# The chunk that spans two batches on the whole array: one group of wide matmuls and a separate multiply of the upper lanes

## The chip, the core and the metric

The program runs on one core of a Trainium2 chip. Its engines work from queues of their own: TensorE (PE, with its weight loads shown as PEld), VectorE (DVE), ScalarE (ACT), GpSimd (POOL) and SyncE (SP), which issues most of the transfers. The metric is the device time of one execution in microseconds (us), lower is better.

## What is computed

The kernel computes a linear attention with random features, and feeds its output to a mixture of experts in which each token goes to one expert. Cut to what matters here:

```python
# q, k, v: (8 batches, 8 heads, 576 tokens, 64); omega: (128 features, 64)
q_p, k_p = phi(q_s), phi(k_s)                     # exp features, 128 per token
kv  = np.einsum('bhsm,bhsd->bhmd', k_p, v)
z   = np.sum(k_p, axis=2)
num = np.einsum('bhsm,bhmd->bhsd', q_p, kv)
den = np.einsum('bhsm,bhm->bhs', q_p, z)[..., None] + 1e-06
attn = num / den
x = attn.transpose(0, 2, 1, 3).reshape(8 * 576, 512)
# then: e = argmax(x @ w_gate); out = gate * sigmoid(...) * (relu(x @ w1[e]) @ w2[e])
```

## The kernel before

**Units.** The attention is done in 32 units. A unit is one head of two batches: 2 times 576 = 1152 tokens, which are 9 chunks of 128. Chunks 0 to 3 belong to the unit's first batch, chunks 5 to 8 to its second, and chunk 4 has 64 tokens of the first and 64 of the second: it spans two batches. Eight units make one of four groups (`j`); after the last unit of a group its tokens are routed to experts, and the expert work is done in items of 128 tokens of one expert (up to 38 of them), whose matmuls stand between those of later units.

**A unit's steps.** `pp` projects keys and queries on PE (L582, 64 rows by 128 columns of the array, in pairs); VectorE takes minima (L604) and makes biases `nb` (L613, L617); ScalarE makes exponentials `ef` (L623); ScalarE and GpSimd split these into a high and a low half-precision part `es` (L644, L646); `kv` sums keys times values on PE (L719); VectorE splits the result into `kvs` (L739, L741); PE multiplies it with the gates (L758, L763); the query features, turned, are `et`. In `kvs` the two batches stand next to each other in the innermost dimension, so that `w[:, :, b]` picks the 81 values of batch b (1 denominator, 64 numerators, 16 gate sums) with a stride of two.

**Numerators.** `attend` (matmuls at L802) multiplies `et` by `kvs` into a PSUM bank `pn`, three products (high-high, high-low, low-high) for each chunk. It is called as two steps: chunks 0 to 4 and chunks 5 to 8. A chunk of one batch takes three matmuls with all 128 columns of weights (128*128 in the rows) and 81 columns streamed. Chunk 4 takes six: three with the weights of its lower 64 tokens against batch 0, written to PSUM lanes 0 to 63, and three with the upper 64 tokens against batch 1, written to lanes 64 to 127. These have 64 columns of weights (128*64 in the rows).

**Division.** `divide` runs on VectorE for each of the two steps: add and scale the denominators (L811), reciprocal (L813), multiply numerators by it into `xf` (L815, 128x400 for chunks 0 to 4, 128x320 for chunks 5 to 8). GpSimd then splits `xf` into rows (L833, L837) and sums gate values (L855; L857 on VectorE at the end of a group).

**Order.** Every step has a number. A table written into the file (`ORDER`) sets the order in which the steps are emitted, a second (`BANKS`) the PSUM bank of each. Each engine executes its instructions in that order and waits where a semaphore says so. The costs given with each step in the code have no effect on that order.

**Items.** An item's hidden layer is at L1586 (`ph`), its second layer at L1617 (`po`, 512 columns streamed), with VectorE's remainder `hl` at L1597 between them. In the last group there are branches for small items, which use 64 columns of weights (L1609).

Of the kernel before, what the change touches and what calls it, by code (L numbers as in the profile page):

```python
# [10 lines left out]
F32 = mybir.dt.float32  # L11
# [4 lines left out]
ALU = mybir.AluOpType  # L16
# [5 lines left out]
P = 128  # L22
B, H, S, D, M = 8, 8, 576, 64, 128
# [3 lines left out]
NSC = 4  # L27
NC = 9
NCV = 10
NP = H // 2  # L30
ROW = DM + 16
KEY = 64
# [3 lines left out]
GW = 2 * NE  # L36
W = 1 + D + GW
# [287 lines left out]
def attention_moe(ctx: ExitStack, tc: tile.TileContext, kqt, kqn, v, om, wg, w1, w2, cf, cm, ci, out):  # L325
    nc = tc.nc
# [44 lines left out]
    def buf(tag, n, shape, dt):  # L371

        n = NBUF.get(tag, n)
        bufs[tag] = n

        def get(i):
            if (tag, i) not in live:
                live[tag, i] = sb.tile([P, *shape], dt, tag=f"{tag}_{i % n}", name=f"{tag}{i}", bufs=1)
            return live[tag, i]

        makers[tag] = get
        return get
# [96 lines left out]
    xl = buf("xlo", 2, [NC * P], F16)  # L479
    rawv = buf("rawv", 2, [NCV, D + 1], F32)  # L480
    vs = buf("vs", 2, [2, NCV, D + 1], F16)
    sqt = buf("sqt", 1, [NC, 2, D], F32)
# [4 lines left out]
    et = buf("et", 2, [2 * NC, P], F16)  # L487
    kvs = buf("kvs", 2, [2, W, 2], F16)
    kvf = buf("kvf", 2, [2, P], F16)
    xf = buf("xf", 2, [NC, D + GW], F32)  # L490
    den = buf("den", 2, [NC], F32)
    xs = buf("xs", 2, [NC, P], F32)
    lga = buf("lga", 2, [NC, GW], F32)

# [38 lines left out]
    def unit(u):  # L533
# [3 lines left out]
        cls = "e" if u < EARLY else "a"  # L537
# [11 lines left out]
        parts = [(g * (NC // 3) * P, (g + 1) * (NC // 3) * P) for g in range(3)] if u == 0 else [(0, NC * P)]  # L549
# [36 lines left out]
        for g in range(G):  # L586
            x = min(g, len(parts) - 1)
            before_ = [("lo", u, x), ("const", "omh")]
            if g or u:
# [3 lines left out]
                tiles=[("xt32", u), ("xn", u)] if whole else [("xhi", u), ("xlo", u)],  # L593
                bank=[(cls, ("pp", 2 * u + i, g), [4, M]) for i in range(2)], cols=3072.0 if whole else 1152.0,
# [3 lines left out]
        for i, nm in enumerate(("k", "q")):  # L598
            n = 2 * u + i
# [27 lines left out]
            for g in range(G):  # L627
# [9 lines left out]
                    tiles=[("nb", n), ("ef", n)], frees=[("pp", n, g)],  # L637
# [32 lines left out]
        if whole:  # L670
# [11 lines left out]
            for g in range(NC // 3):  # L682
                plan.add(
                    ("tq", u, g), ("PE",), 0.33, lambda g=g: turned(g), after=[("ex", qn, g), ("const", "ci")], rank=R + 3,
                    tiles=[("ef", qn)], bank=(cls, ("tq", u, g), [3, P]),
# [3 lines left out]
                    tiles=[("et", u)],  # L689
# [3 lines left out]
                    tiles=[("et", u)], frees=[("tq", u, g)],  # L693
# [11 lines left out]
        def kv_bank():  # L705
            return banks["kv", u][:, 0 : 2 * WIDE * (D + 1)].rearrange("p (b w d) -> p b w d", b=2, w=WIDE)

        def key_values(b):
            kv = kv_bank()
            half = NCV // 2  # L710
            for i in range(half):
# [12 lines left out]
        for b in range(2):  # L724
# [3 lines left out]
                tiles=[("es", slot_es(kn)), ("vs", u)] if fine else [("ef", kn), ("rawv", u)],  # L728
                bank=None if b else (cls, ("kv", u), [512]), cols=1000.0 if fine else 1300.0 * WIDE,
            )  # L730

        def kv_halves(which):
# [14 lines left out]
            tiles=[("kvs", u)],  # L747
# [17 lines left out]
        def gate_halves(which):  # L765
# [12 lines left out]
            tiles=[("kvf", u)],  # L778
# [6 lines left out]
            tiles=[("kvs", u)],  # L785
# [7 lines left out]
        def attend(c0, c1):  # L793
            pn = banks["pn", u, c0]
            kh, kl = (kvs(u)[:, i] for i in range(2))
            eth, etl = et(u)[:, 0:NC], et(u)[:, NC:]
            ops = [(eth, kh), (eth, kl), (etl, kh)]
            for c in range(c0, c1):
                parts = [(0, P, 0 if c < 4 else 1)] if c != 4 else [(0, P // 2, 0), (P // 2, P, 1)]
                for lo, hi, b in parts:  # L800
                    for i, (a, w) in enumerate(ops):
                        nc.tensor.matmul(  # L802
                            pn[lo:hi, c - c0, :], a[:, c, lo:hi], w[:, :, b], start=(i == 0), stop=(i == len(ops) - 1)
                        )

        pr, o = u // 2, (u % 2) * D

        def divide(c0, c1):
            pn = banks["pn", u, c0]
            dn = den(u)[:, c0:c1]  # L810
            nc.vector.tensor_scalar(dn, pn[:, :, 0], EPS * 2.0**LB, 1.0 / SX, ALU.add, ALU.mult)  # L811
            yield
            nc.vector.reciprocal(dn, dn)  # L813
            yield
            nc.vector.tensor_tensor(  # L815
                out=xf(u)[:, c0:c1, :], in0=pn[:, :, 1:], in1=dn.unsqueeze(2).broadcast_to([P, c1 - c0, D + GW]),
                op=ALU.mult,
            )

        for c0, c1, pe, dve in ((0, 5, 0.6, 0.48), (5, NC, 0.42, 0.4)):  # L820
            plan.add(
                ("pn", u, c0), ("PE",), pe, lambda c0=c0, c1=c1: attend(c0, c1), after=[*turned_all, ("gl", u)], rank=R + 5,
                tiles=[("et", u), ("kvs", u)], bank=(cls, ("pn", u, c0), [c1 - c0, W]),
            )
            plan.chain(
                ("xf", u, c0), ("DVE",), (0.07, 0.1, dve), lambda c0=c0, c1=c1: divide(c0, c1), after=[("pn", u, c0)], rank=R + 5,
                tiles=[("xf", u), ("den", u)], frees=[("pn", u, c0)],
            )
# [6 lines left out]
        def lo_half():  # L835
# [7 lines left out]
            tiles=[("xf", u), ("xs", pr)],  # L843
# [6 lines left out]
        def sum_up():  # L850
# [12 lines left out]
            tiles=[("xf", u), ("lga", j)], bank=("e", ("rt", j), [512]) if end else None,  # L863
        )

    def slot_es(n):

        return n // 2 if n < 2 * SPLIT_FROM else n - SPLIT_FROM

    def pair(pr):  # L870
        j, hp = divmod(pr, NP)
        R = 10.0 * (2 * pr + 1) + 7 + GAP * (2 * pr >= H)
        both = [("xl", 2 * pr), ("xl", 2 * pr + 1)]
        plan.add(
            ("rows", pr), ("SP",), 0.45,
            lambda: nc.sync.dma_start(
                rows[j * NC * P : (j + 1) * NC * P, hp * P : (hp + 1) * P].rearrange("(c p) r -> p c r", p=P), xs(pr)
            ),
            after=both, rank=R + 0.5, tiles=[("xs", pr)], dma=1.64,
        )  # L880
# [566 lines left out]
    def cuts_of(n, w, parts=range(NQ)):  # L1447
# [6 lines left out]
        1: [(("ef", FREE + 1), ef), (("ef", FREE + 2), ef), (("et", NSC * H), et), (("et", NSC * H + 1), et)],  # L1454
        2: [(("es", ES), es), (("es", ES + 1), es), (("xs", NSC * NP), xs), (("xs", NSC * NP + 1), xs)],
    }
# [15 lines left out]
    def item(n):  # L1472
# [75 lines left out]
        def gather():  # L1548
# [8 lines left out]
            ("gx", n), "POOL", 1.04, gather, rank=-800.0 + n, tiles=[("gx", n)], dma=0.75,  # L1557
            after=[("gi", gr)] + [("scales", s) for s in range(j + 1)] + [("rows", p) for p in range(NP * (j + 1))],
        )
# [123 lines left out]
    for u in range(NSC * H):  # L1683
        unit(u)
    for pr in range(NSC * NP):
        pair(pr)
# [87 lines left out]
```

## Time and profile before

| what | value |
|---|---|
| time, median of 3 runs | 628.85 us (627.51 to 632.21) |
| the profiled execution's own time | 623.89 us |
| its span, first to last instruction | 622.0 us |
| PE busy | 593.9 us (95%), 8716 matmuls |
| DVE busy | 387.9 us (62%), 1219 instructions |
| ACT busy | 421.6 us (68%) |
| POOL busy | 374.3 us (60%) |
| mean granted clock of TensorE | 0.986 |

The busy time of an engine is the time in which at least one of its instructions is in flight. A matmul is shown from its start until its last result has left the array, and the next one starts long before that; how densely PE works is therefore read from the distance between two starts, not from the length of one. Idle time of an engine that nothing waits for costs nothing.

### The profile page before, as it was taken

Reading aid. Unit: us, or ns where it says so; the run is one execution under the profiler, and the core shown is the slowest. Engines: PE = TensorE matmul, PEld = TensorE weight load, DVE = VectorE, ACT = ScalarE, POOL = GpSimd, SP = SyncE. Lnnn points to the kernel's source line nnn. Section 1 sums busy time; section 2 is a strip of 40 time slices with the busy share of each in tenths; the row PEclk is TensorE's granted clock in tenths of the full one; section 3 lists DMA queues with packets and bytes.
Section 4 is the critical chain, followed back from the end, with each engine's and each line's share of the span. In section 5 each row is a group of like instructions: output and inputs, shape, how many; then the busy total and the mean of one; then the engine's idle time right before and its main releaser. Section 6 shows DMA issues by size and latency. Waiting matters only on the chain. (4 is left out here: it accounts for less than half of the span.)

```text
span 622.0 us, 22247 instructions
## 1 busy us (share of the span) xinstructions
PE 593.9 (95%) x8716; PEld 471.6 (76%) x8716; DVE 387.9 (62%) x1219; ACT 421.6 (68%) x978; POOL 374.3 (60%) x275
## 2 busy tenths in 40 slices
PE   6999987999999899999999999999999999999995
PEld 6999876867786677778877777778867867677764
DVE  4777699866678987647797865543783530351124
ACT  6999999789889688989868787871522521351143
POOL 2265589789976688999788889985322111211203
PEclk9999997899999999999999999999999999999998
DMA  7655689999999999999989998778676647742671
GB/s 269 201 163 167 201 266 210 222 238 268 290 270 249 225 252 209 289 199 230 298 223 260 231 196 200 175 180 212 203 163 215 205 80 215 203 99 55 132 284 50
DMA packets 145888, 129.00 MB, mean 207 GB/s; under 512 B 104270, under 2 KB 127440, under 8 KB 144464
## 3 DMA queue, kind: packets, MB, share of 16 engines
q1 hardware_dynamic: 139760, 107.45, 69.1%
q0 software_dynamic: 5984, 19.72, 10.3%
q8 instruction: 80, 1.31, 0.9%
q14 instruction: 64, 0.52, 0.3%
HBM read 83.86 MB, written 19.30 MB: 166 GB/s over the span
## 5 line engine op out<-in xcount | busy, mean ns | idle before, releaser
L1586 PE MATMUL ph<-xt,w1h 128*128 128x128 f16 (+1 forms) x2432 | 206.8, 218 | 0.8 <-ACTq L1510 0.4
L1586 PE MATMUL ph<-xt,w1l 128*128 128x128 f16 (+1 forms) x1216 | 203.1, 218 | 0.4 <-DVEq L1515 0.4
L1586 PEld LDWEIGHTS <-w1h 128*128 128x128 f16 x2432 | 184.3, 98 | 9.0 <-issue 1.3
L623 ACT ACTIVATE ef<-pp,nb 128x128 f32<-128x128 f32 x576 | 163.0, 394 | 17.3 <-DVE nb L617 13.1
L604 DVE TENSOR_REDUCE pp<-pp 128x3 f32<-128x384 f32 x192 | 102.8, 557 | 33.2 <-PE pp L582 28.2
L1586 PEld LDWEIGHTS <-w1l 128*128 128x128 f16 x1216 | 118.5, 98 | 0.5 <-DVEq L1515 0.5
L646 POOL TENSOR_TENSOR es<-ef,es 128x1152 f16<-128x1152 f32 x44 | 104.5, 2385 | 20.1 <-ACT es L644 13.4
L1597 DVE SCALAR_TENSOR_TENSOR hl<-ph,hh 128x512 f16<-128x512 f32 (+1 forms) x76 | 50.4, 664 | 97.8 <-ACTq L1515 61.4
L1617 PE MATMUL po<-w2h,hl 128*128 128x512 f16 x280 | 106.1, 379 | 1.8 <-DVE hl L1597 1.8
L1617 PE MATMUL po<-w2h,hh 128*128 128x512 f16 x280 | 106.2, 379 | 0.2 <-PE ph L1586 0.2
L1617 PE MATMUL po<-w2l,hh 128*128 128x512 f16 x280 | 106.1, 379 | 0.0
L1549 POOL DMA_INDIRECT gx<-rows,gi x38 | 38.2, 1005 | 104.4 <-ACT os L1672 46.1
L1593 ACT ACTIVATE hh<-ph 128x512 f16<-128x512 f32 (+1 forms) x76 | 44.6, 590 | 83.0 <-PE ph L1586 69.3
L1617 PEld LDWEIGHTS <-hh 128*128 128x128 f16 x560 | 51.3, 98 | 52.7 <-issue 0.3
L516 POOL TENSOR_TENSOR xlo<-xt,xhi 128x1152 f16<-128x1152 f32 x24 | 57.2, 2383 | 10.8 <-ACT xhi L509 8.6
L1617 PEld LDWEIGHTS <-hl 128*128 128x128 f16 x280 | 27.4, 98 | 35.4 <-DVE hl L1597 2.5
L1672 ACT ACTIVATE os<-po,gx 128x512 f32<-128x512 f32 (+1 forms) x34 | 23.4, 687 | 43.8 <-PE po L1617 37.6
L644 ACT CAST es<-ef 128x1152 f16<-128x1152 f32 x44 | 51.5, 1181 | 0.7 <-ACTq L1510 0.2
L802 PE MATMUL pn<-kvs,et 128*128 128x81 f16 (+1 forms) x960 | 47.5, 204 | 0.9 <-ACT ef L623 0.5
L802 PEld LDWEIGHTS <-et 128*128 128x128 f16 (+1 forms) x960 | 40.5, 101 | 7.6 <-issue 0.5
L582 PE MATMUL pp<-omh,xhi 64*128 64x128 f16 x432 | 42.6, 223 | 2.9 <-ACT ef L623 1.9
L582 PE MATMUL pp<-omh,xlo 64*128 64x128 f16 x432 | 41.1, 222 | 0.7 <-POOL xlo L516 0.7
(193 smaller groups left out, 1059.6 us busy)
## 6 DMA issues: line engine op xcount, KB each, us to landing
r<-w SPq DMA_DIRECT2D x10, 2048.0 KB, 9.0
xt<-kqt SPq DMA_DIRECT2D x32, 576.0 KB, 5.3
xn<-kqn SPq DMA_DIRECT2D x24, 576.0 KB, 5.7
rawv<-v SPq DMA_DIRECT2D x32, 325.0 KB, 5.4
rows<-xs SPq DMA_DIRECT2D x16, 576.0 KB, 6.0
r<-w SPq DMA_DIRECT2D x8, 512.0 KB, 6.3
ef<-w SPq DMA_DIRECT2D x2, 512.0 KB, 3.9
et<-w SPq DMA_DIRECT2D x2, 512.0 KB, 8.0
```

What stands on the lines that cost most here:

```text
L516: lambda t0=t0, t1=t1: nc.gpsimd.tensor_tensor(out=xl(u)[:, t0:t1], in0=xt32(u)[:, t0:t1], in1=xh(u)[:, t0:t1], op=ALU.subtract),
L582: nc.tensor.matmul(banks["pp", 2 * u + i, g][:, c, :], x[r, t], w[r, :], start=(a == 0), stop=(a == len(ops) - 1))
L604: nc.vector.tensor_reduce(out=pp[:, 3, 0:3], in_=pp[:, 0:3, :], op=ALU.min, axis=AX.X)
L623: nc.scalar.activation(ef(n)[:, c, :], banks["pp", n, g][:, c % 3, :], AF.Exp, bias=nb(n)[:, c : c + 1], scale=-SK)
L644: nc.scalar.copy(es(slot_es(n))[:, 0], ef(n))
L646: nc.gpsimd.tensor_tensor(out=es(slot_es(n))[:, 1], in0=ef(n), in1=es(slot_es(n))[:, 0], op=ALU.subtract)
L802: nc.tensor.matmul(pn[lo:hi, c - c0, :], a[:, c, lo:hi], w[:, :, b], start=(i == 0), stop=(i == len(ops) - 1))
L1549: nc.gpsimd.indirect_dma_start(out=gx(n), out_offset=None, in_=rows[0 : (j + 1) * NC * P], in_offset=bass.IndirectOffsetOnAxis(ap=tabs[gr] ...
L1586: nc.tensor.matmul(ph[:, f4, 0:w_], w[qd][:, kk, fo : fo + P], xt(n)[:, x, 0:w_], start=(a == 0), stop=(a == 3 * KC - 1))
L1593: nc.scalar.activation(hh(n)[:, sl, 0:w_], banks["ph", n, g][:, :, 0:w_], AF.Relu)
L1597: nc.vector.scalar_tensor_tensor(out=hl(n)[:, sl, 0:w_], in0=banks["ph", n, g][:, :, 0:w_], scalar=0.0, in1=hh(n)[:, sl, 0:w_], op0=ALU.ma ...
L1617: nc.tensor.matmul(po, x(n)[:, f, :], w[f // 2][:, f % 2, :], start=(f == 0 and a == 0), stop=(f == FC - 1 and a == 2))
```

## The change

From unit 10 on, chunk 4 is no longer cut at lane 64. Its three products use all 128 columns of weights and stream 162 columns, the 81 of both batches, into two neighbouring blocks of the bank: block 4 holds batch 0's result for all 128 lanes, block 5 batch 1's. Half of each block isn't used. The bank grows from 5 blocks to 6, the denominators of the step from 5 to 6, and `den` from 9 to 10. The multiply of chunks 0 to 4 stays as it is and now writes wrong values to lanes 64 to 127 of chunk 4; a second VectorE multiply of 64 lanes by 80 values, from block 5, writes these lanes again. In units 0 to 9 nothing changes. The tables of the order and of the banks are the same.

```diff
+MID = NC // 2
+ABREAST = 10
...
-    den = buf("den", 2, [NC], F32)
+    den = buf("den", 2, [NC + 1], F32)
...
             for c in range(c0, c1):
-                parts = [(0, P, 0 if c < 4 else 1)] if c != 4 else [(0, P // 2, 0), (P // 2, P, 1)]
+                if c == MID and abreast:
+                    for i, (a, w) in enumerate(ops):
+                        nc.tensor.matmul(
+                            pn[:, c - c0 : c - c0 + 2, :], a[:, c], w.rearrange("p w b -> p b w"), start=(i == 0), stop=(i == len(ops) - 1)
+                        )
+                    continue
+                parts = [(0, P, 0 if c < MID else 1)] if c != MID else [(0, P // 2, 0), (P // 2, P, 1)]
...
         pr, o = u // 2, (u % 2) * D
+        abreast = u >= ABREAST
+
+        def blocks(c0, c1):
+            return c1 - c0 + (abreast and c0 <= MID < c1)
 
         def divide(c0, c1):
             pn = banks["pn", u, c0]
-            dn = den(u)[:, c0:c1]
+            n = blocks(c0, c1)
+            dn = den(u)[:, c0 + (c0 > MID) :][:, 0:n]
             nc.vector.tensor_scalar(dn, pn[:, :, 0], EPS * 2.0**LB, 1.0 / SX, ALU.add, ALU.mult)
             yield
             nc.vector.reciprocal(dn, dn)
             yield
             nc.vector.tensor_tensor(
-                out=xf(u)[:, c0:c1, :], in0=pn[:, :, 1:], in1=dn.unsqueeze(2).broadcast_to([P, c1 - c0, D + GW]),
+                out=xf(u)[:, c0:c1, :], in0=pn[:, 0 : c1 - c0, 1:], in1=dn[:, 0 : c1 - c0].unsqueeze(2).broadcast_to([P, c1 - c0, D + GW]),
                 op=ALU.mult,
             )
+            if n > c1 - c0:
+                nc.vector.tensor_tensor(
+                    out=xf(u)[P // 2 :, MID, :], in0=pn[P // 2 :, n - 1, 1:], in1=dn[P // 2 :, n - 1 : n].broadcast_to([P // 2, D + GW]), op=ALU.mult
+                )
...
-                tiles=[("et", u), ("kvs", u)], bank=(cls, ("pn", u, c0), [c1 - c0, W]),
+                tiles=[("et", u), ("kvs", u)], bank=(cls, ("pn", u, c0), [blocks(c0, c1), W]),
```

On PE, the end of unit 10's step for chunks 0 to 4 stands like this before, from the last full chunk to the next step (the first number of a MATMUL row's shape is the lanes that it writes, the second the columns streamed):

```order
L802 LDWEIGHTS et_2328
L802 MATMUL pn_0_2590<-kvs_2212,et_2328 128x81
L802 LDWEIGHTS et_2328
L802 MATMUL pn_0_2590<-kvs_2212,et_2328 64x81
L802 LDWEIGHTS et_2328
L802 MATMUL pn_0_2590<-kvs_2212,et_2328 64x81
...
L802 LDWEIGHTS et_2328
L802 MATMUL pn_0_2590<-kvs_2212,et_2328 64x81
L763 LDWEIGHTS kvf_2555
L763 MATMUL kv_2386<-wgs,kvf_2555 128x32
```

The same place on PE in the changed kernel:

```order
L810 LDWEIGHTS et_2328
L810 MATMUL pn_0_2590<-kvs_2212,et_2328 128x81
L803 LDWEIGHTS et_2328
L803 MATMUL pn_0_2590<-kvs_2212,et_2328 128x162
L803 LDWEIGHTS et_2328
L803 MATMUL pn_0_2590<-kvs_2212,et_2328 128x162
L803 LDWEIGHTS et_2328
L803 MATMUL pn_0_2590<-kvs_2212,et_2328 128x162
L765 LDWEIGHTS kvf_2555
L765 MATMUL kv_2386<-wgs,kvf_2555 128x32
```

Six narrow matmuls with their weight loads have become three wide ones; what stands ahead and behind is the same. Of the 22 changed units, 9 have a projection (L584 of the changed kernel, L582 before, 64 rows of the array) right behind the three, the other 13 an instruction that uses the whole array. On VectorE, the division of the same unit stands like this before (what is in brackets is the engine whose semaphore the instruction waits for):

```order
L811 TENSOR_SCALAR den_2628<-pn_0_2590 128x5 [waits PE_49]
L813 RECIPROCAL den_2628<-den_2628 128x5 [waits DVE_49]
L815 TENSOR_TENSOR xf_2629<-pn_5_2577,den_2628 128x320 [waits Pool_49]
L1597 SCALAR_TENSOR_TENSOR hl_2490<-ph_1_2494,hh_2464 128x512 [waits Activation_49]
L815 TENSOR_TENSOR xf_2629<-pn_0_2590,den_2628 128x400 [waits DVE_49]
L617 SCALAR_TENSOR_TENSOR nb_2479<-pp_2_2558,sqs_2279 128x3
```

And so in the changed kernel:

```order
L824 TENSOR_SCALAR den_2625<-pn_0_2590 128x6 [waits PE_49]
L826 RECIPROCAL den_2625<-den_2625 128x6 [waits DVE_49]
L828 TENSOR_TENSOR xf_2626<-pn_5_2577,den_2625 128x320 [waits Pool_49]
L1614 SCALAR_TENSOR_TENSOR hl_2490<-ph_1_2494,hh_2464 128x512 [waits Activation_49]
L828 TENSOR_TENSOR xf_2626<-pn_0_2590,den_2625 128x400 [waits DVE_49]
L833 TENSOR_TENSOR xf_2626<-pn_0_2590,den_2625 64x80 [waits DVE_49]
L619 SCALAR_TENSOR_TENSOR nb_2479<-pp_2_2558,sqs_2279 128x3
```

One instruction has been put behind the multiply of chunks 0 to 4, and it waits for that multiply to be finished. The order of all else on VectorE is the same, and GpSimd, ScalarE and SyncE have the same instructions in the same order.

## Rows read from the trace of the kernel before

**Rows 1.** The page: busy us, share of the span, instructions.

```profile
PE 593.9 (95%) x8716; PEld 471.6 (76%) x8716; DVE 387.9 (62%) x1219; ACT 421.6 (68%) x978; POOL 374.3 (60%) x275
```

**Rows 2.** Windows: busy us (count) of each engine, PEclk the granted clock.

```profile
100.00:107.00 7.00, 5.11 (x46) 5.01 (x46) 6.86 (x37) 5.78 (x16) 7.00 (x4) 0.74 0.71 193
107.00:113.90 6.90, 6.69 (x73) 5.75 (x71) 5.33 (x23) 5.21 (x15) 3.36 (x3) 0.51 1.01 218
...
120.00:445.00 325.00, 318.99 (x5123) 249.30 (x5122) 228.48 (x760) 258.23 (x591) 266.02 (x189) 1.00 0.97 235
```

**Rows 3.** Waits of PE from 120 to 445 us: total, times, longest.

```profile
PE po L1617 <- DVE hl L1597: 1.8, 1, 1.8
...
PE kv L758 <- DVE nb L617: 1.1, 1, 1.1
PE kv L719 <- POOL es L646: 0.9, 2, 0.6
```

**Rows 4.** Timeline of PE at units 19 and 21: start, us, instructions merged.

```profile
268.03 0.88 PE L802 MATMUL pn<-kvs,et 128*128 128x81 f16 x18
268.84 0.28 PE L1586 MATMUL ph<-xt,w1h 128*128 128x128 f16 x2
...
282.19 0.28 PE L1586 MATMUL ph<-xt,w1h 128*128 128x128 f16 x2
282.30 0.22 PE L1586 MATMUL ph<-xt,w1l 128*128 128x128 f16 x1
282.35 0.28 PE L758 MATMUL kv<-cmt,kvs 128*128 128x128 f16 x2
282.56 0.23 PE L582 MATMUL pp<-omh,xhi 64*128 64x128 f16 x2
...
283.67 0.64 PE L802 MATMUL pn<-kvs,et 128*128 128x81 f16 x12
284.15 0.23 PE L763 MATMUL kv<-wgs,kvf 128*128 128x32 f16 x3
...
286.91 0.87 PE L802 MATMUL pn<-kvs,et 128*128 128x81 f16 x18
287.71 0.23 PE L582 MATMUL pp<-omh,xhi 64*128 64x128 f16 x2
```

**Rows 5.** Groups of VectorE's instructions, 127 to 445 us: busy, mean ns.

```profile
L815 DVE TENSOR_TENSOR xf<-pn,den 128x400 f32<-128x400 f32 x22 | 12.4, 567 | 0.4
L815 DVE TENSOR_TENSOR xf<-pn,den 128x320 f32<-128x320 f32 x22 | 10.6, 484 | 0.4
```

**Rows 6.** The same view, 470 to 475 us: the multiply-like row on 64 lanes.

```profile
L1261 DVE TENSOR_TENSOR r_gid<-r_gid,a_g_a_i_n 64x24 f32<-64x24 f32 x1 | 0.2, 183 | 1.9 <-PE a_g_a_i_n L1257 1.9
```

**Rows 7.** Timeline of VectorE, then of PE, around 202 to 209 us.

```profile
202.22 0.57 DVE L815 TENSOR_TENSOR xf<-pn,den 128x400 f32<-128x400 f32 x1
202.71 0.30 DVE L741 SCALAR_TENSOR_TENSOR kvs<-kv,kvs 128x130 f16<-128x130 f32 x1
202.91 4.12 DVE L857 TENSOR_TENSOR rt<-lga,xf 128x144 f32<-128x144 f32 x1
206.94 0.55 DVE L604 TENSOR_REDUCE pp<-pp 128x3 f32<-128x384 f32 x1
...
206.13 0.38 PE L1617 MATMUL po<-w2l,hh 128*128 128x512 f16 x1
208.35 0.39 PE L1617 MATMUL po<-w2h,hl 128*128 128x512 f16 x1 [1.83 <-DVE hl L1597]
```

**Rows 8.** Timeline of VectorE at the routing after unit 31.

```profile
444.35 0.23 DVE L929 TENSOR_REDUCE r_top<-rt 128x9 f32<-128x72 f32 x1
444.62 0.24 DVE L933 TENSOR_TENSOR rt<-rt,r_top 128x72 f32<-128x72 f32 x1
```

**Rows 9.** Timeline of GpSimd, 204 to 207 and 365 to 371 us.

```profile
204.46 2.38 POOL L516 TENSOR_TENSOR xlo<-xt,xhi 128x1152 f16<-128x1152 f32 x1
...
367.65 2.39 POOL L646 TENSOR_TENSOR es<-ef,es 128x1152 f16<-128x1152 f32 x1
```

## The prediction

> **What bounds the kernel now.** I read the busy shares first, then who waits for whom on PE, then PE's timeline around a changed step. The shares say that PE works 95% of the span and VectorE 62% [rows 1]; in the stretch that holds all changed steps, 120 to 445 us, PE has an instruction in flight for 318.99 of 325 us at full clock, VectorE for 228.48 and GpSimd for 266.02 [rows 2]. So PE is the bound and its order is fixed: an instruction that PE doesn't execute is time won, unless PE then comes early to a wait that another engine ends. The few such waits in this stretch are the second view: 1.8 us on VectorE's `hl`, 1.1 us on VectorE's biases, 0.9 us on GpSimd's `es` in two waits [rows 3]. They are short, but so is all that this change can give; the forecast hangs on them.
>
> **What the six narrow matmuls cost.** A step of one-batch chunks only is 12 matmuls, and PE starts the next step 0.48 us after its first (283.67 to 284.15), so 0.040 us for one of 81 columns. A step with chunk 4 is 18, and lasts 0.81 us before a full-array successor (268.03 to 268.84) and 0.80 before a projection (286.91 to 287.71) [rows 4]. Less the 12 full ones (0.48), the six narrow ones take 0.33 us, far more than six such streams side by side need. Part of it is the change of the array's shape: two matmuls of 128 columns take 0.21 us until a projection on 64 rows starts (282.35 to 282.56), where three among their like take 0.16 (282.19 to 282.35), 0.055 each; so going over to another shape costs 0.21 - 0.11 = 0.10 us [rows 4]. Chunk 4 pays this on the way in and on the way out: 0.20, and 0.13 us of streaming.
>
> [...]
>
> **What the three wide ones cost.** No row has 162 columns. Taken from 81 and 128 columns (0.040 and 0.055 us) the line goes to 0.066; two of 81 one after the other would be 0.080 [rows 4]. I take 0.07, so 0.21 us for three (0.20 to 0.24), the ends being these two. The stride of two in the streamed operand is there before too. Weights are loaded as for a full chunk.
>
> **PE's sum.** In 13 of the 22 changed units the successor uses the whole array: both shape changes go, 0.33 - 0.21 = 0.12 us each, 1.56 us. In 9 a projection follows, and going over to its 64 rows still costs the 0.10: 0.33 - 0.21 - 0.10 = 0.02 us, 0.2 us together. That is 1.8 us off PE's queue. With 0.24 for the three it is 13 x 0.09 - 9 x 0.01 = 1.1 us; if the last shape change hid behind the wide streams and three took 0.20, 22 x 0.13 = 2.9 us.
>
> **VectorE's sum.** One multiply of 64 lanes by 80 values is added in each of 22 units. Multiplies of 400 and 320 values take 567 and 484 ns, 1.04 ns for each further value [rows 5]; a row on 64 lanes with 24 values takes 183 ns [rows 6], so 80 values come to 183 + 56 x 1.04 = 241 ns. The sixth block adds one value each to two small instructions, a few ns. The multiply waits for the one ahead of it: a row that follows unhindered starts some 0.08 us before the end of the one ahead (202.71 against 202.22 + 0.57) [rows 7], one that waits for its predecessor some 0.04 after it (444.62 against 444.35 + 0.23) [rows 8]. So the queue behind gets later by 0.24 + 0.04 = 0.28 us, by 0.36 if the row behind starts without overlap as well; 22 of them are 6.2 to 7.9 us of VectorE's time. Queued behind are minima, biases, `hl` and the splits of weights; for the multiply itself GpSimd's row split waits. No transfer is moved.
>
> [...]
>
> **What of it reaches the end.** VectorE's 6.2 us are spread over 325 us of which it is idle for 96 [rows 2]. PE waits for it at two places only. The longer is at 208.35, where PE waits 1.83 us for `hl`. VectorE sits there 4.12 us in one small addition (L857, from 202.91) and goes on at 206.94, just when GpSimd's `es` and `xlo` have ended (204.46 + 2.38 = 206.84) [rows 7, 9]. That release is GpSimd's: VectorE arriving 0.3 or 0.6 us later in front of it changes nothing, and PE arriving earlier wins nothing. So the savings of units 10 to 15, 4 x 0.12 + 2 x 0.02 = 0.5 us, are gone there. The 1.1 us wait for the biases [rows 3], which comes after unit 17, takes those of units 16 and 17 (0.14) in the same way, if the biases stay where they are. GpSimd, at 82% in this stretch, ends two more waits (0.9 us, the later one on the `es` from 367.65) [rows 2, 3, 9]; between the wait for the biases and that last one units 18 to 26 save 4 x 0.12 + 5 x 0.02 = 0.58 us, of which I count half. Units 27 to 31 save 4 x 0.12 + 0.02 = 0.5 us with nothing behind them but items, and that PE keeps. Together 0.5 + 0.3 = **0.8 us**. The routing after unit 31 gets its input 0.3 us later on VectorE, but items lie in PE's queue meanwhile, and this costs nothing; were that cover gone, it would be 0.3 us.
>
> The sum is against the profiled execution: 623.89 - 0.8 = 623.1 us. The median of the runs is 5.0 us above that execution with the same instructions; I put the same difference on it: 628.85 - 0.8 = **628.0 us**.
>
> **Rivals.**
> - All of PE's saving arrives. Then the waits on VectorE and GpSimd move forward along with PE, since their inputs come from PE's projections. For it: VectorE itself waits for PE at many places. Against: the release at 206.94 is GpSimd's. 628.85 - 1.8 = 627.0 us, at the bound 626.0.
> - VectorE's multiply gets on the path: slower. The place is the stretch between a unit's projection and its exponentials, where `nb` stands behind the added row and ScalarE, then GpSimd, then PE wait in turn. It decides as soon as more than 0.08 us (1.8 / 22) of the 0.28 per unit reaches PE. If half does, 22 x 0.14 - 1.8 = +1.3 us, 630.2; if all does, 6.2 - 1.8 = +4.4 us, 633.3, or 6.1 more with 0.36 (634.9). Against: PE waits for VectorE for 2.9 us in two waits only [rows 3].
> - Narrow was the better shape. In pairs of column tiles the six would stream in 3 x 0.040 = 0.12 us, and three wide ones in 0.21: +0.09 us each, 22 x 0.09 = +2.0 us, 630.9. This holds if the shape changes are hidden behind something; the 0.33 us for six [rows 4] speak against it. [...]
> - The clock. From 107 us the granted clock stands at 0.51 for 6.9 us, after a stretch in which PE was busy 5.11 of 7 us and at 0.74 [rows 2]. Work at half clock for 6.9 us costs 3.4 us. One such stretch more or fewer gives 631.4 or 624.6. It lies ahead of unit 10, in code that isn't changed, and PE isn't as idle again before 445 us.
> - The change does not do what it says if the wide form were to run at less than one column a step; with twice the 0.07, 0.42 us, it would lose 13 x 0.09 + 9 x 0.19 = 2.9 us, 631.7.
>
> **Chances and range.** The forecast 0.52; all arrives 0.18; VectorE on the path 0.18; narrow better or wide slow 0.05; the clock 0.07, half each way. Runs of the same kernel lie 4.7 us apart, and 1% (6.3 us) is about what a measurement of this kernel can tell from no change. No case but the far end of VectorE's comes near it on the slow side, and none on the fast side without help of the clock: faster by over 1% 0.02, within 0.95, slower 0.03. The range goes from 624.8 (one stretch of low clock fewer, or all arriving plus the spread of the runs) to 632.0 (half to two thirds of VectorE's cost arriving).
>
> **What the profile will show.** PE at L803: three wide matmuls some 0.07 us apart, and steps of 0.69 us where 0.81 stood, 0.79 ahead of a projection. PE has 66 matmuls fewer, VectorE 22 instructions more at 0.24 us, 5.3 us of busy time. The wait at 208 us gets longer by about 0.5 us and ends at the same time; from unit 27 on PE is ahead by up to 0.8 us. I am wrong if PE's waits for VectorE's biases or `hl` grow by more than 2 us in total, if the wide matmuls start more than 0.09 us apart, or if the clock falls at another place.

## The result

The changed kernel takes 634.99 us (median of 20 runs, 631.26 to 640.76), the kernel before 627.88 (20 runs). The ratio is 1.0095, 95% interval 1.0076 to 1.0114: about 6 us slower, where 0.8 us faster was forecast. Some executions fall into a slower state whatever the kernel, and every ratio here is estimated without them, so it is not the quotient of the medians.

The profiled execution took 636.24 us (span 634.5). The profile of before that was shown is of an execution 4 us below its median, so the spans of the two profiles lie 12.5 us apart where the medians lie 7.1 apart. A second profile of before (below) shows which of the differences are chance.

First the parts that came out as forecast. Busy shares of the changed kernel (the page's first part; instructions are behind the x):

```profile
PE 596.6 (94%) x8650; PEld 472.6 (74%) x8650; DVE 394.0 (62%) x1241; ACT 422.4 (67%) x978; POOL 373.9 (59%) x275
```

PE has 66 matmuls fewer than in [rows 1], VectorE 22 instructions more. The groups of the added multiply (L833 in the changed kernel) and of the wide matmuls (L803), with the least, median and longest duration in ns:

```profile
L833 DVE TENSOR_TENSOR xf<-pn,den x22: 244/244/245, 131.7 to 448.7; 64x80 f32<-64x80 f32 x22
```
```profile
L803 PE MATMUL pn<-kvs,et x66: 234/237/242, 129.3 to 443.9; 128*128 128x162 f16 x66
```

The multiply takes 244 ns (forecast 241). PE's timeline around a step with chunk 4, which answers to [rows 4]:

```profile
281.96 0.63 PE L810 MATMUL pn<-kvs,et 128*128 128x81 f16 x12
282.43 0.39 PE L803 MATMUL pn<-kvs,et 128*128 128x162 f16 x3
282.65 0.28 PE L1603 MATMUL ph<-xt,w1h 128*128 128x128 f16 x2
```

Twelve full matmuls, three wide ones 0.07 to 0.08 us apart, and the next step 0.69 us after the first (0.69 to 0.74 before the other full-array successors); ahead of a projection, which follows nine times as forecast, it is 0.79 where nothing waits. The prices of PE's instructions were right. The granted clock is at half speed (0.50) for 6.8 us from 108.0 us on, about as in [rows 2], and in this profile once more, for 3.4 us from 261.6 us on (the stretch, its length, busy time and count of each engine, then the clock):

```profile
260.00:270.00 10.00, 9.30 (x131) 7.39 (x132) 6.74 (x23) 6.58 (x17) 7.52 (x5) 0.83 0.92 223
```

The prediction had named a clock that falls at another place as a sign of being wrong, and here is one. In those 3.4 us matmuls of 81 columns start 0.068 us apart and those of 65 columns 0.055, where the medians from 120 to 261 us are 0.040 and 0.029; that is not quite twice, so the stretch can account for 1.7 us of this profile at most; what PE did ahead of it is told in the last section. The rest of the loss is elsewhere. PE's waits from 120 to 445 us (engine, line, waited for: total, times, longest), which answer to [rows 3], and then those of the items' stretch behind:

```profile
PE kv L760 <- DVE nb L619: 1.4, 1, 1.4
PE ph L1603 <- ACT os L1689: 1.0, 1, 1.0
PE pp L584 <- DVE hl L1614: 1.0, 1, 1.0
PE pn L810 <- DVE nb L619: 0.9, 1, 0.9
PE pp L584 <- DVEq L1527: 0.8, 2, 0.5
```
```profile
PE ph L1603 <- issue: 3.8, 4, 1.4
PE ph L1603 <- DMA xt<-gx: 2.0, 2, 1.1
PE ph L1603 <- ACTq L1532: 1.3, 1, 1.3
```

Two things are new. Up to 445 us VectorE (DVE, and DVEq for its queue) now ends seven groups of waits, 5.1 us in all (the four of them shown here are 4.1), where it ended two with 2.9 us; the longest of before, 1.8 us for `hl`, is gone. Behind that, where nothing of the change executes, PE stands for 3.8 us in "issue", which no semaphore explains. I compare two stretches by the start of the same matmul in each timeline: the **units' stretch**, from the projection at 117.0 us to the second-layer product at 444.2 (times of before), and the **items' stretch**, from there to the end of the span. In the shown profile of before they take 327.2 and 177.8 us, in the changed kernel 331.7 and 185.2. Each is one execution, and other profiles of kernels without the change will show how far chance moves these numbers.

### The profile page after: what moved, and what is told of

It is laid out like the page before. It is cut to its first block, busy times and chain, and to the rows that moved or that the text cites. A ratio compares the mean times of both kernels' runs of the same rounds, so it can differ in the third digit from the quotient of the medians.

```text
span 634.5 us, 22136 instructions
## 1 busy us (share of the span) xinstructions
PE 596.6 (94%) x8650; PEld 472.6 (74%) x8650; DVE 394.0 (62%) x1241; ACT 422.4 (67%) x978; POOL 373.9 (59%) x275
## 5 line engine op out<-in xcount | busy, mean ns | idle before, releaser
L584 PE MATMUL pp<-omh,xhi 64*128 64x128 f16 x432 | 43.8, 224 | 4.6 <-DVE hl L1614 1.0
L810 PE MATMUL pn<-kvs,et 128*128 128x81 f16 (+1 forms) x828 | 42.5, 203 | 2.6 <-DVE nb L619 0.9
L584 PEld LDWEIGHTS <-xhi 64*128 64x128 f16 x864 | 33.9, 97 | 12.8 <-issue 4.7
L810 PEld LDWEIGHTS <-et 128*128 128x128 f16 (+1 forms) x828 | 36.6, 99 | 8.1 <-issue 2.6
```

What stands on the lines that cost most here:

```text
L584: nc.tensor.matmul(banks["pp", 2 * u + i, g][:, c, :], x[r, t], w[r, :], start=(a == 0), stop=(a == len(ops) - 1))
L810: nc.tensor.matmul(pn[lo:hi, c - c0, :], a[:, c, lo:hi], w[:, :, b], start=(i == 0), stop=(i == len(ops) - 1))
```

## The experiments

Two theories. A: the 22 multiplies are on the path, in the units. B: the 132 instructions that PE no longer has (66 matmuls, 66 weight loads) move all its later code, and the fetching of instructions then stalls PE at other places. C, chance, is the rival to both.

### The multiplies alone, PE's saving alone

`dve_only` is the kernel before with, behind L815,

```diff
+            if u >= 10 and c0 == 0:
+                nc.vector.tensor_tensor(
+                    out=xf(u)[P // 2 :, 4, :], in0=pn[P // 2 :, 4, 1:], in1=dn[P // 2 :, 4:5].broadcast_to([P // 2, D + GW]), op=ALU.mult
+                )
```

> The kernel before, PE untouched, with only the second multiply of the upper 64 lanes of the middle chunk added in units 10 to 31 (it writes the values that are there already). Theory A, that VectorE's 22 extra instructions are on the path of the units: PE reaches the end of the units (444 us in the trace before) 5 to 7 us later, and the whole is 1.008 to 1.011 of the kernel before. Theory B, that the loss is one of where PE's code lies and not of VectorE: PE's code is the same as before, so the end of the units moves by under 1 us and the whole stays within 0.3%. Theory C, that the two profiles differ by chance: within 0.3% too.

Measured: 1.0081 (1.0049 to 1.0113). The units' stretch takes 333.2 us, the items' 181.3. The interval and the units' stretch are what theory A expects. PE's longest waits for VectorE from 120 to 445 us:

```profile
PE kv L758 <- DVE nb L617: 1.8, 1, 1.8
PE pn L802 <- DVE nb L617: 1.1, 1, 1.1
PE pp L582 <- DVE hl L1601: 1.0, 1, 1.0
```

`pe_only` is the changed kernel without the `if n > c1 - c0:` block (the second multiply).

> The changed kernel without the second multiply: the upper 64 lanes of the middle chunk keep the first batch's quotient in units 10 to 31, so those tokens get wrong values and may be routed to other experts; only the time up to the end of the units is comparable. Theory A: what is left is the saving on PE, so the end of the units comes 0 to 1.8 us earlier than 444 us. Theory B: PE's code is that of the changed kernel, so the end of the units comes as late as there, about 449 us.

Measured, one profile: PE reaches the last step comparable (404.9 us in before) 289.4 us behind the mark at 117; in six profiles of kernels without the change it is 285.1 to 289.0. The forecast saving on PE is not to be seen; neither is the loss of 4 us that the changed kernel has by then (292.1). Behind 405 us it executes other items, so its 655.8 us mean nothing.

### Shifting code

PE's and VectorE's queues begin with a wait of 3.6 and 3.4 us. Drains placed there move the code behind them, and as long as they fit, they hardly delay the first step: with 48 the first matmul starts at 4.98 us (`after_pad48`), without any at 4.89 (the changed kernel). At 0.07 us each, the price that the two kernels below give, 52 of PE's fit. The edit, ahead of the first step:

```diff
+        for _ in range(48):
+            nc.tensor.drain()
         emit(0)
```

`before_pad124` and `after_pad132` have 124 and 132 of them. These don't fit: the first matmul comes 4.8 and 5.3 us later, (3.6 + 4.8) / 124 = 0.07 us for each drain and as much with 132.

The count of 256 in the two expectations below can be read from the traces: from the packet of 16,384 bytes on the instruction queue that starts at 120.70 us in the profile of before to the one at 444.92 there are 40 such packets, and PE executes 10,249 instructions, 256 for each; in the changed kernel (119.61 to 442.05 us) 39 packets and 9905 instructions, 254. From one packet to the next it is 140 to 421 in before, so 256 is a mean.

> The kernel before with 124 drains of PE at the program's start, while PE has nothing to do: its later code lies, in blocks of 256 instructions, where the changed kernel's lies behind unit 31 (132 instructions fewer there). Theory A: no effect, within 0.3% of the kernel before, or up to 0.4 us more for the drains themselves. Theory B: the items' stretch (444 us to the end) gets the stalls of the changed kernel, 1.0 to 1.5 us each with no semaphore behind them, 5 to 9 us in the sum, and the whole is 1.006 to 1.014. Theory C: within 0.3%, with stalls of that kind at places of their own.

> The changed kernel with 132 drains of PE at the start: its later code lies, in blocks of 256 instructions, where that of the kernel before lies behind unit 31. Theory A: no effect, 1.0076 to 1.0114 as the changed kernel. Theory B: the items' stretch loses the stalls without a semaphore, 5 to 8 us, and the whole falls to 0.997 to 1.003 of the kernel before if the units cost nothing, or to about 1.004 if half of the loss lies there. Theory C: as the changed kernel, with stalls at other places.

Measured: 1.0122 (1.0085 to 1.0160) and 1.0104 (1.0071 to 1.0137). I had put the drains' own cost at 0.4 us, which was wrong, so the totals say little; the items' stretch does: 184.0 and 180.8 us, where the unpadded kernels took 177.8 and 185.2. In these two it goes with the code's place and not with the change.

`before_again` is the kernel before, unchanged.

> The kernel before once more, unchanged, for a second profile. If the stalls in the items' stretch (444 us to the end, 177.8 us in the first profile) belong to PE's code position, this profile shows those of the kernels with the same position (0.37, 0.65, 0.36 and 0.67 us at the same matmuls) and the stretch takes 180 to 181.5 us; if they are chance, 177 to 184 us with stalls at other matmuls. Between 117 and 444 us it takes 325 to 328 us and VectorE does not stand for 1.7 us in front of the denominators at 256 us, under either.

Measured: 627.76 us; 328.6 and 179.6 us. Stalls of 0.34, 0.66, 0.35 and 0.52 us stand at the expected matmuls, the last one three further. The first profile of the same kernel has none of the four, so the place of the code alone doesn't fix these short ones. The expectation on VectorE missed: it stood in front of the denominators for 1.9 us here too, and the wait for `hl` at 208 us on which a term of the forecast rested is absent:

```profile
PE ph L1586 <- DVE sqs L527: 1.7, 1, 1.7
PE pn L802 <- DVE nb L617: 1.2, 1, 1.2
PE pp L582 <- DVE hl L1597: 1.0, 1, 1.0
PE kv L758 <- DVE nb L617: 0.8, 1, 0.8
```

`after_pad48`, `after_pad24` and the control `before_pad48` have drains that fit; `before_vpad11` and `before_vpad22` have 11 and 22 of VectorE's.

> The changed kernel with 48 drains of PE at the start, which fit into the 3.6 us in which PE waits there: PE's later code lies 48 instructions on. If PE's code position makes the stalls without a semaphore in the items' stretch, they stand at other matmuls or are of other sizes than 1.2, 1.6, 1.1, 0.5 and 1.5 us, and the stretch differs from 185.2 us by more than 2 us; the stretch from 117 to 444 us stays at 329 to 333 us. If position does nothing, the stalls are as in the changed kernel, and the whole within 0.3% of it.

> The changed kernel with 24 drains of PE at the start in place of 48. If PE's code position sets the stalls in the items' stretch, these stand elsewhere or have other sizes than with 0 and with 48 drains, and the time lies anywhere from 1.002 to 1.011, most likely between those two kernels; with the drains as such as the cause it is half way, 1.006.

> The kernel before with 48 drains of PE at the start, in time that PE waits there anyway. Control for the changed kernel with the same drains, which came out 5 us faster than without them. If the drains help by themselves (a later start, the clock, the transfers), this kernel gains about as much: 0.991 to 0.995. If they work only through the place of PE's code, this kernel has no bad place to leave: 0.997 to 1.004, with the items' stretch at 177 to 184 us.

> The kernel before with 11 drains of VectorE at the program's start, where it waits for 3.4 us anyway: its code lies 11 instructions later, as it does in the changed kernel around unit 20, and it does no more work. Theory A (the extra multiplies are on the path): no effect, within 0.3%. Theory B' (VectorE's code position makes its 1.7 us stall in front of the denominators at 259 us): the stall is here too, the stretch from 210 to 260 us takes 51 to 52 us in place of 48.5 to 49.1, and the whole is 1.003 to 1.006.

> The kernel before with 22 drains of VectorE at the start, where it waits for 3.4 us: its code lies where that of the changed kernel lies behind unit 31, and it does no more work. If VectorE's code position makes the 0.8% that the added multiplies alone cost, this kernel is 1.005 to 1.010; if it is their work in the units, 0.996 to 1.002.

| kernel | ratio to before | units' stretch | items' stretch | lost inside hidden layers |
|---|---|---|---|---|
| changed kernel | 1.0095 (1.0076 to 1.0114) | 331.7 | 185.2 | 6.5 |
| after_pad24 | 1.0089 (1.0057 to 1.0121) | 330.7 | 186.7 | 6.3 |
| after_pad48 | 1.0033 (1.0002 to 1.0064) | 328.6 | 180.2 | 2.4 |
| before_pad48 | 1.0038 (1.0006 to 1.0069) | 327.2 | 186.3 | 3.8 |
| before_vpad11 | 0.9971 (0.9948 to 0.9993) | 327.7 | 186.4 | 3.3 |
| before_vpad22 | 1.0013 (0.9978 to 1.0047) | 324.6 | 181.3 | 2.3 |

48 drains that do nothing take back two thirds of the loss, and before gains nothing from the same 48 (1.0038, the upper half of what was expected; with 48 drains in both, the kernel with the change and the one without it come out alike). `after_pad48`'s units' stretch lies 0.4 us under the expectation. No cost of VectorE's code place is seen, in the units as little as behind. (Both 186.3 and 186.4 hold a late transfer near 593 us, PE waiting 2.5 and 2.8 us for an item's rows `xt`. That wait comes and goes among the profiles, so a single items' stretch is read with care.)

The table's last column leaves such waits out. It adds up, in us, what PE loses between two neighbouring matmuls of one hidden-layer step in the items' stretch, wherever their starts lie over 0.3 us apart, where 0.056 us is regular (0.5 us of it is one wait for VectorE's queue that all of them have). It is 6.5 in the changed kernel, 6.3 with 24 drains and 5.8 in `before_pad124`. In ten profiles whose PE code lies there as before's does, with the change or without it (`after_pad132` 2.8, `wide_split` below 3.0), it is 2.2 to 3.3, and in the first profile of before 0.5. The changed kernel thus loses 3.2 to 4.3 us more than those ten in a stretch where it executes the same work. PE's waits in that stretch that no semaphore explains, 3.8 us above, are 1.0 us in `before_again` and in `after_pad48` these:

```profile
PE ph L1603 <- issue: 1.2, 4, 0.4
```

What the drains move is seen in one step, the same hidden layer of one item, in the changed kernel and with 24 and 48 drains (timelines of PE; first the step's first row, then the row behind the stall):

```profile
498.77 0.28 PE L1603 MATMUL ph<-xt,w1h 128*128 128x128 f16 x2
...
502.33 0.23 PE L1603 MATMUL ph<-xt,w1l 128*128 128x128 f16 x1 [1.40 <-issue]
```
```profile
497.16 0.28 PE L1603 MATMUL ph<-xt,w1h 128*128 128x128 f16 x2
...
500.15 0.23 PE L1603 MATMUL ph<-xt,w1l 128*128 128x128 f16 x1 [1.44 <-issue]
```
```profile
493.96 0.28 PE L1603 MATMUL ph<-xt,w1h 128*128 128x128 f16 x2
...
494.88 0.23 PE L1603 MATMUL ph<-xt,w1l 128*128 128x128 f16 x1 [0.29 <-issue]
```

Counted in the full timelines, the stall stands behind 32, 20 and 8 matmuls of the step: each 24 drains move it 12 matmuls forward, which with their weight loads are 24 instructions. It is tied to a place in PE's code. Each trace also holds a packet of 16,384 bytes on the instruction queue ahead of the stall's end: these land at 500.95, 498.78 and 493.50 us, and PE goes on 1.38, 1.37 and 1.38 us later. PE's last branch instruction stands 1.3 us ahead of the step in all three (497.49, 495.88, 492.69). In these three, how long PE runs dry goes with where the place lies behind the branch: 32 and 20 matmuls in, the packet starts only within the step (500.01, 497.82) and PE loses 1.6 us; 8 in, it starts ahead of it (492.56), and PE loses 0.5. A later step has the same: a stall behind 24 matmuls without drains (551.54 us; it is the row of 1.3 us above, which the profile puts down to ScalarE's queue), behind 12 with 24.

`before_pad124` bears the 256 out in part: its 124 drains and the 132 instructions that the change takes away make 256 together, a packet's mean count, and it has stalls of 1.6 and 1.6 us behind the same matmuls of two steps as the changed kernel (1.1 and 1.5 there), though not the one shown above. That it is the branch which makes a packet late is argued from the three steps; no run tests it by itself.

### The change with the code in its old place

`wide_split` keeps the wide shape and the multiply, but not the fewer instructions:

```diff
-                    for i, (a, w) in enumerate(ops):
-                        nc.tensor.matmul(
-                            pn[:, c - c0 : c - c0 + 2, :], a[:, c], w.rearrange("p w b -> p b w"), start=(i == 0), stop=(i == len(ops) - 1)
-                        )
+                    for b in range(2):
+                        for i, (a, w) in enumerate(ops):
+                            nc.tensor.matmul(pn[:, c - c0 + b, :], a[:, c], w[:, :, b], start=(i == 0), stop=(i == len(ops) - 1))
```

`abreast24_pad48` is the changed kernel with `ABREAST = 24` and 48 drains: 8 units changed, code in place.

> The changed kernel with each whole-array matmul of 162 columns split into two of 81, one for each batch: six matmuls and six weight loads as before, so PE's code lies exactly where that of the kernel before does, while the wide shape and VectorE's second multiply stay. Position theory: the items' stretch is 178 to 181.5 us in place of 185, and the whole 1.002 to 1.008, the cost of the multiplies alone. If the place of the code does nothing and the loss is the multiplies' and the wide shape's: 1.009 and more, with the stretch at 184 to 187 us.

> The change in units 24 to 31 alone, 48 PE instructions fewer, made good by 48 drains in PE's idle start: behind unit 31 its code lies exactly where that of the kernel before does. If the change as such is nearly neutral there, 0.997 to 1.003; if the multiplies cost on every unit what 22 of them cost alone, 8 of them are 1.003, less up to 0.001 for PE's saving.

Measured: 1.0032 (0.9996 to 1.0068) and 0.9985 (0.9950 to 1.0020). `wide_split`'s units' stretch is 329.8 us, its items' stretch 182.9 (1.4 over the expectation; it holds one wait of 1.5 for `xt`). For `abreast24_pad48` they are 328.5 and 184.7, the latter with 2.5 for `xt`. In `wide_split` a step with chunk 4 takes 0.70 to 0.75 us before a full-array successor, as in the changed kernel (0.69 to 0.74), so both have the same saving on PE, and they differ in the place of the code. Six instructions more on PE in each unit, no work less, and 0.63% of the 0.95% are gone (interval about 0.2 to 1.0%, from the intervals of the two): 3.9 us.

### How many multiplies cost how much

`dve_twice` issues the added multiply twice, `dve_early` only in units 10 to 19, `dve_late` only in 20 to 31.

```diff
-            if u >= 10 and c0 == 0:
+            for _ in range(2 if u >= 10 and c0 == 0 else 0):
```

> The kernel before with the second multiply added twice over in units 10 to 31: 44 instructions more on VectorE, 10.6 us of its time, PE untouched. If their work is on the path as the single one's 0.8% says, twice as much is 1.013 to 1.020, and the stretch from 117 to 444 us takes 336 to 340 us in place of 326 to 329. If the single one's cost was position or chance, 1.000 to 1.009.

> The kernel before with the second multiply added in units 10 to 19 alone (10 of the 22). If the cost lies where VectorE is full of the routings' steps (210 to 260 us), 1.005 to 1.008, nearly all of the 1.0081; if every multiply costs the same, 1.0037.

> The kernel before with the second multiply added in units 20 to 31 alone (12 of the 22). If the cost lies in units 10 to 19, 0.999 to 1.002; if every multiply costs the same, 1.0044.

Measured: 1.0087 (1.0056 to 1.0119), 1.0038 (1.0002 to 1.0073), 1.0020 (0.9988 to 1.0052). Double is less than twice single. Early and late don't decide: early is what an even share predicts, but its interval takes in the 1.005 to 1.007 of a cost in units 10 to 19 too, and late stands at the end of the one expectation and holds the other in its interval. A straight line through zero over the five kernels that have 10, 12, 22, 22 and 44 multiplies with PE's code in place (`wide_split` among them, which has PE's saving as well) gives 0.48% for 22, 3.0 us; each fits it within its interval, `dve_only` by a hair not.

The line is a price, not a mechanism, and the profiles don't show an even share. The units' stretch is 335.7 us in `dve_twice`, just under the expected 336 to 340, 331.5 and 330.7 in the other two, and 324.6 to 328.6 in the six profiles without any of the change. One part of it, between two projections that start at 211.5 and 259.5 us in the first profile of before, comes in two lengths (`act_mul` aside): 47.4 to 50.0 us in seven profiles, 50.8 to 52.4 in ten. Two of the ten, `before_again` and `dve_late`, have executed no added multiply by then; the last section tells what happens there. The rest of the units' stretch is 277.2 to 279.8 us in the six without the change and 277.7 to 279.3 in the five that have all of it in all 22 units (the changed kernel, its three with drains, `wide_split`). So with the whole change, the loss up to 444 us is seen at this one place only. The rest is 282.1 in `dve_only` and 284.4 in `dve_twice`, which have the multiplies and not PE's saving (280.5, 279.9 and 280.9 in `dve_early`, `dve_late` and `abreast24_pad48`). That is a hint that the multiplies cost a little everywhere and PE's saving pays for it, but these are single profiles, and no run tests it.

### The multiply on ScalarE

```diff
-                nc.vector.tensor_tensor(
-                    out=xf(u)[P // 2 :, MID, :], in0=pn[P // 2 :, n - 1, 1:], in1=dn[P // 2 :, n - 1 : n].broadcast_to([P // 2, D + GW]), op=ALU.mult
-                )
+                nc.scalar.activation(xf(u)[P // 2 :, MID, :], pn[P // 2 :, n - 1, 1:], AF.Copy, scale=dn[P // 2 :, n - 1 : n])
```

> The changed kernel with the second multiply of the upper 64 lanes done by ScalarE, as a copy with a scale, in place of VectorE. Theory A: VectorE's part of the loss, 3 to 5 us between 117 and 444 us, goes, and ScalarE's 22 copies of 0.25 us cost 0 to 2 us; 1.001 to 1.006 of the kernel before. Theory B: PE's position is that of the changed kernel, so its 3.5 us in the items' stretch stay. Rival: ScalarE then waits for the reciprocal in the middle of its queue and holds up the exponentials behind it; 1.010 and more.

Measured: 1.0442 (1.0391 to 1.0494). The rival, far beyond its price. The stalls in the items' stretch stand behind the same matmuls as in the changed kernel, as theory B says. The copy takes 0.32 us, but ScalarE stands in front of it (waits of ScalarE, 120 to 445 us):

```profile
ACT xf L833 <- DVE xf L828: 16.5, 8, 3.9
ACT xf L833 <- DVE nb L619: 10.7, 4, 4.1
```

No version beats both kernels: only `before_vpad11`, which changes nothing but a start, has its interval below 1, and its sister with 22 drains doesn't.

## Why the prediction was wrong

- **The sum on PE** held in its prices: 0.69 to 0.74 and 0.79 us steps, 0.07 us wide matmuls, nine successors that are projections. That 1.8 us of PE's queue become time was not shown by any run: `pe_only` has no lead, and 3.9 us for the code and 3.0 for the multiplies leave 0.9 of the 6.0 us, well inside the intervals. It stays open.
- **The code behind the change** is the step that failed most. The prediction let units 27 to 31 save 0.5 us "with nothing behind them but items, and that PE keeps", and put the items themselves at nothing; of transfers it said that none is moved. The packets with PE's own code are transfers too, one for some 256 of its instructions, and 132 instructions fewer move all its later code; with 48 drains to move it again the stalls among the items stood elsewhere and were shorter (2.4 us lost in place of 6.5). That the branches there make the difference is an inference. Price 3.9 us (1.4 to 6.5) by the totals, of which the kept profiles show 3.2 to 4.3 in the items' stretch, where the change executes nothing. This was in no rival.
- **"PE waits for it at two places only"** was the step that hid VectorE's 6.2 us. It read a list of PE's waits as the room that VectorE has; a wait that is absent because VectorE is just in time doesn't stand in it. Measured 3.0 us for 22 multiplies. The rival's "if half does" had +3.1 on VectorE's side and a chance of 0.18, but the agreement is luck: it meant half of 0.28 us in each unit, and with the whole change the profiles show the loss at one place, near 256 us. The rival's far end, 634.9 us, meets the measured 635.0 by luck too, since more than half of the loss is the code's. The sign given for VectorE didn't show: PE's waits for the biases and `hl` came to 3.3 us after 2.9, not to 2 more. The list of waits was also short of its second longest, on exponentials that VectorE's biases release:

```profile
PE pp L582 <- ACT ef L623: 1.2, 1, 1.2
```

- **The 0.28 us of one multiply** were too few. The prediction left open whether the row behind it would start without the overlap of 0.08 us (0.36). It does, and starts later still: in the changed kernel the row behind begins 0.01 to 0.03 us after the multiply's end in 20 of 22 units (after a wait in the other two), as in the rows below. That makes up to 0.03 + 0.24 + 0.03 + 0.08 = 0.38 us for each, 8.4 us for 22 in place of 6.2.

```profile
131.10 0.56 DVE L828 TENSOR_TENSOR xf<-pn,den 128x400 f32<-128x400 f32 x1
131.70 0.24 DVE L833 TENSOR_TENSOR xf<-pn,den 64x80 f32<-64x80 f32 x1
131.98 0.17 DVE L619 SCALAR_TENSOR_TENSOR nb<-pp,sqs 128x3 f32<-128x3 f32 x1
```

- **The wait at 208 us.** 0.5 us of PE's saving were given away to a release by GpSimd [rows 7]. Of the profiles without the change only the first shows that wait; the stretch from 166 to 210 us, 44.5 us there, is 42.4 to 43.6 in the five others. A chance event was taken for a fixture.
- **The clock** and **the narrow shape** as rivals: the mark behind the half-speed stretch at 107 us comes at 117.7 us in the changed kernel, 117.0 to 118.2 in the five kernels without the change whose first matmul isn't delayed, so nothing of the loss lies there; the second stretch at half speed, at 261 us, is in the shown profile and, at 265, in `after_pad132`, but `after_pad24`, `after_pad48` and `wide_split` have none between 115 and 445 us. The narrow shape wasn't better: its steps take 0.80 to 0.83 us before a full-array successor where the whole-array steps take 0.69 to 0.75. In the step of before that starts at 268.03 us its matmuls do start in pairs, 0.010 us apart, but 0.13 us lie between the last full one and the first of them, and 0.13 from the last to the successor, where 0.040 is regular: the shape changes are not hidden.

In sum: +3.9 us code, +3.0 us VectorE, PE's saving unresolved, against +6.0 measured. The first two are estimates from different runs, and their sum is no more exact than their intervals.

## What to carry over

Taking 132 instructions out of PE, the bound of this program, moved its later code, and that alone was worth about 0.6% (0.2 to 1.0%): before a change under 1% is judged, shift the code by some drains in an idle start (24 and 48 gave 1.0089 and 1.0033) and compare at an equal place. VectorE's 30% of idle time was no cover by itself (22 multiplies cost 3.0 us); ask at which instruction such an engine is just in time. And a wait that a term rests on should be seen in two profiles.

## What was unexpected of the hardware

**VectorE late beside a gather and a scatter of GpSimd.** At 256 us VectorE's denominators wait for PE's `pn`. In the first profile of before, then in `dve_only` (timeline; POOL's DMA_INDIRECT rows are the gather and the scatter):

```profile
255.03 0.64 PE L802 MATMUL pn<-kvs,et 128*128 128x81 f16 x12
255.71 0.16 DVE L811 TENSOR_SCALAR den<-pn 128x4 f32<-128x4 f32 x1 [2.75 <-issue]
255.71 0.99 POOL L1549 DMA_INDIRECT gx<-rows,gi  x1
257.01 1.02 POOL L1659 DMA_INDIRECT out<-os,oi  x1 [0.30 <-issue]
```
```profile
255.92 0.99 POOL L1553 DMA_INDIRECT gx<-rows,gi  x1 [0.15 <-issue]
256.53 0.65 PE L802 MATMUL pn<-kvs,et 128*128 128x81 f16 x12
257.22 1.03 POOL L1663 DMA_INDIRECT out<-os,oi  x1 [0.30 <-issue]
258.89 0.16 DVE L811 TENSOR_SCALAR den<-pn 128x4 f32<-128x4 f32 x1 [4.42 <-remote]
```

In before `pn` is ready at 255.67 and VectorE starts 0.04 us later. In `dve_only` `pn` is ready at 257.18, in the middle of the pair, and VectorE starts at 258.89, 0.65 us after the scatter's end. Over 17 profiles it is one or the other: `pn` ready up to 0.48 us behind the gather's start (7 of 17), and VectorE begins within 0.2 us; ready 0.77 us or more behind it (10 of 17), and VectorE begins 0.51 to 0.68 us behind the scatter's end, 1.5 to 2.1 us late. All eight kernels in which VectorE has executed added multiplies by then are on the late side, of the nine others two (`before_again`, and `dve_late`, whose multiplies come later). The eighteenth profile, `act_mul`, fits neither: ready 0.72 us behind the gather's start, VectorE begins 1.35 us later, 0.26 us before the scatter's end. In the changed kernel PE then stands for 1.9 us in three pieces at the next projections (until 260.31, 261.07 and 261.60 us), and the clock is at half speed from 261.6 us. The part of the units' stretch around this place takes 47.4 to 50.0 us in the seven early profiles and 50.8 to 52.4 in the ten late ones, 51.3 and 50.8 in the two late ones without multiplies: about 3 us. This is how a delay of half a microsecond may cost three, and perhaps why the second multiply of `dve_twice` cost little more than the first. That the two rows on GpSimd hold VectorE is inferred from the times; it was not tested.

**Stalls that go with instruction packets** (PE goes on 1.37 to 1.38 us after one lands) cost up to 1.6 us each in the steps shown, on an engine that had nothing else to wait for. The place of such a stall moved with a count of instructions, 12 matmuls for 24 drains; the short ones come and go between two profiles of one kernel.
